# Two attention-and-routing stages on one core: the bank sum before the pair's last sum, the copy before a relu, and another order in the first item

## The chip, the cores and the metric

One core of a Trainium2 chip runs the whole program in one launch. The time is the device time of one execution in microseconds (us). The times shown are the median of several executions on the chip, and one further execution was recorded with its profile.

## The reference, cut to what matters

```python
x = attention(q, k, v, S1, S2)                  # (4352, 128): polynomial-sketch attention
P = exp(x @ w_gate - max)                       # 4352 x 8 gates
for _ in range(8):                              # Sinkhorn: rows, then columns
    P /= P.sum(1, keepdims=True) + 1e-09
    P /= P.sum(0, keepdims=True) + 1e-09
    P *= N / E
for e in range(8):                              # every token through every expert
    h = np.maximum(x @ w1[e], 0.0)              # 128 -> 1024
    out += P[:, e:e + 1] * (h @ w2[e])          # 1024 -> 128
```

Everything is fp32. All eight experts see all 4352 tokens, so the expert part is two dense products per token and expert.

## The kernel before, in words

**Two phases.** Up to about 194 us of the profile the kernel does the attention, the gates and some expert work (`steps`, lines 779 to 824). From then on `weighted` (lines 953 to 1262) does the rest: 60 *items*, each a group of tokens with one expert. The gate is multiplied into x ahead of the first layer, which a relu lets through because gates are positive.

**Groups, items and halves.** `wgroups` (line 592) has ten groups of tokens. Groups 0 to 4 have two blocks of 256 tokens and seven experts, groups 5 to 7 two blocks of 224 and six, group 8 five and group 9, `LAST`, two. An item is run in two *halves* (s = 0 and 1: which half of the hidden columns). `todo` (line 960) lists the halves as t = 0, 1, 2 and so on, so item 0 is t = 0 and 1, and item 1 is t = 2 and 3.

**Two layers, interleaved.** The loop at line 1240 runs `firsts(t)`, the first layer of half t, against `seconds(t - 1)`, the second layer of the half before, one `yield` of each in turn. A *slot* below is one such turn on TensorE: eight matmul records of the profile, either of line 986 (first layer) or of line 1124 (second layer). Seven first-layer slots and seven second-layer slots make a half.

**Fewer products by sums (groups 1 to 8 in both layers, items 1 and up in the first).** The first layer of a half has two token blocks and two column blocks, which need eight block products. `firsts` does seven, of sums of weights (`w1x`, eight forms; `sum_first` makes four of them on GpSimd once per expert) and of sums of tokens (`xf`, eight forms; `sum_x` makes four of them per item, in three parts). The seven go by turns into two PSUM tiles, `pairs[0]` and `pairs[1]`, called `pa` and `pc` in a half. ScalarE copies three partial results out (`p1`, `p5`, `u2`; lines 1061, 1067, 1070), and VectorE adds them back (`add`, line 990): h0 after the fourth product, h2 after the fifth, **h3, the pair's last sum, after the sixth**. ScalarE does the relu (line 993) of h0, of h2 and, after the seventh, of h1. VectorE then makes four sums for the second layer from h1 and h3 (lines 1086, 1095, 1096, 1097). Since `pa` and `pc` swap with t, the first product of half t + 1 goes into the tile that h3's add of half t reads.

**Item 0 is direct.** Its sums of weights aren't made yet, so it does eight plain products (lines 1047 to 1059): four results of two products each, with a relu on ScalarE after each second one. In item 0 the tiles alternate within a half and swap between halves as everywhere, so the last result of t = 0 and the first of t = 1 share a tile, and so do the last of t = 1 and the first product of t = 2.

**The end of a group.** The second layer adds up in four PSUM banks, `acc[g][rho][q]`. The next group uses the same four banks, so its first second-layer slot waits until they are read. For groups 1 to 8, while `seconds` runs the group's last half in slots 0 to 6, `firsts` of the next group's first half runs beside it. After second-layer slot 3 `ended(g, 0)` copies bank (0, 0) to the tile `z` on ScalarE (line 1170), and `ending` holds g. At first-layer slot 5 `add_half(g, 0)` adds bank (1, 0) to it on VectorE (line 1175): this is **the bank sum**. The other two banks follow at the end (`ended(g, 1)`, `add_half(g, 1)`). Group 0, whose second layer is direct, does all of this in its last slot. `z` has one buffer. `finish_seven` puts nine adds that read z and a swapped copy of it on a list, `leisure`, and later halves do them one at a time, on VectorE in `spare` and on GpSimd in `aside`.

**Queues.** Each engine runs its instructions in the order in which `weighted` writes them, SyncE its DMAs too. SyncE's queue around item 0 is: the swapped copy of item 2's x (`weigh`, line 904), the store of expert 1's weight sums (`store_form`, line 887, two parts), the load of w2 for item 1 (`prepare(1, True)`, line 860), the store of item 1's first sums (line 887), and the load of w1 for item 2 (line 856, four DMAs). Each store waits for GpSimd's sums; each DMA behind it in the queue waits with it. The ACT copies of line 1003 are one column wide and only hold GpSimd's work back until a point of the half (`gate`).

Of the kernel before, what the change touches and what calls it, by code (L numbers as in the profile page):

```python
# [50 lines left out]
def kernel(  # L51
# [825 lines left out]
    def sum_second(i):  # L877
        _, w2, ws = forms[i]
        g = nc.gpsimd
        four = [ws[:, n].rearrange("p (r s) d -> p r s d", r=2) for n in range(4)]  # L880
        g.tensor_tensor(four[0], block_of(w2, 1, 0), block_of(w2, 1, 1), op=Alu.add)
        g.tensor_tensor(four[1], four[0], block_of(w2, 0, 0), op=Alu.subtract)
        g.tensor_tensor(four[2], block_of(w2, 1, 0), block_of(w2, 0, 0), op=Alu.subtract)
        g.tensor_tensor(four[3], block_of(w2, 0, 1), four[1], op=Alu.subtract)

    def store_form(i, which):
        nc.sync.dma_start(out=form_stores[witems[i][1]][which], in_=forms[i][2 * which])
# [65 lines left out]
    def weighted():  # L953
# [16 lines left out]
        def firsts(t):  # L970
# [1 line left out]
            i, s = todo[t]  # L972
            g, e = witems[i]
            n = wgroups[g][1]
            a, c = pairs[t % 2], pairs[1 - t % 2]
            w1, xf = forms[i][0], sources[i]
            h, ts = rooms(t)
            pa, pc = a[:, :, 0:n], c[:, :, 0:n]
# [10 lines left out]
            def add(out, x, y):  # L989
                nc.vector.tensor_tensor(flat(out, n), x, flat(y, n), op=Alu.add)  # L990

            def relu(x, y):
                nc.scalar.activation(out=x, in_=y, func=Act.Relu)  # L993
# [11 lines left out]
            def aside(y):  # L1005


                if s == 0 and i + 2 < len(witems):
                    weigh(i + 2, lambda x: gate(x, y))
                if s == 1 and i + 1 < len(witems) and g:  # L1010
                    gate(sources[i + 1][:, 4, 0:1], y)
                    sum_x(i + 1, 0)
                if g == 0:
                    nexts = i + 1 < len(wgroups[0][2])
                    if s == 0:
                        if nexts:
                            gate(forms[i + 1][0][:, 4, 0:1], y)
                            sum_first(i + 1)
                        if i == 0:
                            sum_first(0)  # L1020
                            sum_second(0)
                            store_form(0, 0)
                        store_form(i, 1)
                    elif nexts:
                        gate(forms[i + 1][2][:, 0, 0, 0:1], y)
                        sum_second(i + 1)
                        store_form(i + 1, 0)
                elif chores and (s or not leisure):
                    chores.pop(0)[1]()
                else:  # L1030
                    leave(nc.gpsimd)
# [15 lines left out]
            if i == 0:  # L1047
                for out, (fi, ti), b in ((pa, (0, 1), 0), (pc, (1, 0), 1), (pa, (1, 1), 2), (pc, (0, 0), 3)):
                    for k in range(2):
                        product(out, 2 * k + fi, 2 * k + ti, k == 0, True)  # L1050
                        if k:
                            relu(flat(h[:, b], n), out)
                        if b == 0 and k:
                            aside(h[:, b, 0:1])
                        if b == 3 and k:
                            for part_ in ((1, 2) if s else (0,)):
                                sum_x(1, part_)
                        yield
                return
# [12 lines left out]
            yield  # L1072
            product(pc, 7, 3, False, True)
            add(h[:, 0], pc, u2)
            relu(h[:, 0], h[:, 0])
            yield
            product(pa, 6, 5, False, True)
            add(h[:, 2], pa, p5)
            relu(h[:, 2], h[:, 2])
            yield  # L1080
            product(pc, 2, 2, True, True)
            add(h[:, 3], pc, p1)
            if g in whole:
                relu(h[:, 3], h[:, 3])
            else:
                nc.vector.scalar_tensor_tensor(ts[:, 0], h[:, 3], 0.0, h[:, 0], op0=Alu.max, op1=Alu.subtract)  # L1086
            if ending:
                add_half(ending[0], 0)
            else:
                spare(0)  # L1090
            yield
            product(pa, 3, 7, False, True)
# [147 lines left out]
        for t in range(len(todo) + 1):  # L1240
            if t < len(todo):
                i, s = todo[t]
                g0 = witems[i][0]
                if s == 0:
                    prepare(i + 1, False)
                    if i + 3 < len(witems):
                        load_weights(i + 3)
                    if i == 0:
                        chores += chores_of(0) + chores_of(1)
                    if i and witems[i - 1][0] < g0 and g0 + 1 < LAST:  # L1250
                        chores += chores_of(g0 + 1)
                else:
                    prepare(i + 1, True)
            f = firsts(t) if t < len(todo) else iter(())
            s = seconds(t - 1) if t else iter(())
            nothing_, open_ = object(), 2
            while open_:
                open_ = sum(next(x, nothing_) is not nothing_ for x in (f, s))
# [108 lines left out]
```

## Time and profile before

| | |
|---|---|
| median of 3 executions | 911.18 us (910.59 to 912.69) |
| the profiled execution's own time | 910.05 us |
| its span, first to last instruction | 908.3 us |
| TensorE granted clock | 1.00 of full speed |
| VectorE, ScalarE, GpSimd busy | 721.9, 548.9, 245.2 us |
| TensorE weight loads busy | 703.5 us |
| HBM read and written | 137.24 and 19.57 MB |

In the timeline a row is: start, duration, engine, line, operation, output and inputs, shape, and in brackets the idle time of the engine just before and what ended it. Neighbouring instructions of one kind are merged (x8 is eight of them). The waits view has: engine and line, what it waited for, total us, times, longest. TensorE's matmuls overlap one another, so the idle time that a row shows is less than the time lost; the distance between equal instructions of two halves gives the loss. The copy of u2 (line 1070) comes once in each half, a fixed distance behind the third first-layer slot, and serves as such a beat.

### The profile page before, as it was taken

How to read it: one execution, taken by the hardware profiler on the slowest of the kernel's cores; microseconds unless marked ns; L12 is line 12 of the kernel's file. 1: busy time of each engine (PE TensorE's matmuls, PEld its weight loads, DVE VectorE, ACT ScalarE, POOL GpSimd, SP SyncE). 2: the span in 40 equal slices, each digit the busy share in tenths (PEclk: the TensorE clock that was granted, in tenths of full speed). 3: DMA queues.
4: the chain of work that ended last, by engine and by line, in shares of the span. 5: the costliest groups of instructions: out<-in, count | busy, mean ns of one | idle time of the engine just before them, and what ended most of it. 6: DMA issues, size and time to landing. Idle time of an engine off the chain costs nothing.

```text
span 908.3 us, 35879 instructions
## 1 busy us (share of the span) xinstructions
PE 895.1 (99%) x15484; PEld 703.5 (77%) x15484; DVE 721.9 (79%) x1268; ACT 548.9 (60%) x1092; POOL 245.2 (27%) x297
## 2 busy tenths in 40 slices
PE   9999999999999999999999999999999999999997
PEld 5777644557887766788877777888999978999996
DVE  7578789874445888888888888888898888888885
ACT  2446465646665666666666666666666666666664
POOL 3121100045652322233223222222233222233220
PEclk9999999999999999999999999999999999999999
DMA  8996200148885676485757667755884974875863
GB/s 240 291 277 201 54 1 1 49 110 290 265 239 194 219 240 198 128 268 189 223 183 236 182 205 208 240 190 152 257 258 129 291 257 117 275 242 165 281 202 90
DMA packets 124782, 177.98 MB, mean 196 GB/s; under 512 B 28976, under 2 KB 94720, under 8 KB 117584
## 3 DMA queue, kind: packets, MB, share of 16 engines
q1 hardware_dynamic: 121920, 170.18, 60.4%
q0 software_dynamic: 1600, 5.36, 2.1%
q8 instruction: 122, 2.00, 0.9%
q10 hardware_dynamic: 1104, 0.15, 0.1%
q14 instruction: 36, 0.29, 0.1%
HBM read 137.24 MB, written 19.57 MB: 173 GB/s over the span
## 4 chain that ended last, share of the span: by engine, by line
PE 84%; issue 10%; DVE 2%; POOL 1%; DMA 1%; ACT 1%; SPq 0%; POOLq 0%; DVEq 0%; ACTq 0%
PE s L1124 37%; PE pair L986 36%; PE a L711 4%; PE s L772 3%; PE a L305 1%; PE a L118 1%; PE a L420 1%; DMA w<-in_moe_w_dram 1%; DVE hb L990 1%; DVE hb L1086 1%; DVE z L1175 0%; PE a L272 0%; DMA pb<-pT 0%; PE s L334 0%; POOL xf L901 0%
## 5 line engine op out<-in xcount | busy, mean ns | idle before, releaser
L986 PE MATMUL pair<-xf,w1x 64*64 64x256 f32 (+1 forms) x6736 | 603.4, 366 | 2.0 <-ACT xf L1003 1.0
L986 PEld LDWEIGHTS pair<-xf,w1x 64*64 64x64 f32 x6736 | 337.8, 133 | 55.7 <-ACT hb L993 1.9
L990 DVE TENSOR_TENSOR hb<-pair,copies 128x512 f32<-128x512 f32 (+1 forms) x354 | 234.7, 663 | 127.7 <-PE pair L986 53.4
L1124 PE MATMUL s<-hb,w 64*64 64x256 f32 (+1 forms) x3600 | 312.4, 366 | 3.4 <-DVE z L1175 2.8
L1124 PE MATMUL s<-hb,ws 64*64 64x256 f32 (+1 forms) x3264 | 300.6, 364 | 0.0
L993 ACT ACTIVATE hb<-hb 128x512 f32<-128x512 f32 (+1 forms) x252 | 153.3, 609 | 112.2 <-DVE hb L990 107.6
L1124 PEld LDWEIGHTS s<-hb,w 64*64 64x64 f32 x3600 | 185.0, 133 | 38.7 <-PE pair L986 4.0
L1124 PEld LDWEIGHTS s<-hb,ws 64*64 64x64 f32 x3264 | 180.7, 133 | 27.7
L901 POOL TENSOR_TENSOR xf<-xT,pb 128x512 f32<-128x512 f32 (+1 forms) x60 | 75.2, 1254 | 302.1 <-ACT xf L1003 213.3
L910 POOL TENSOR_TENSOR xf<-xf 128x512 f32<-128x512 f32 (+1 forms) x52 | 63.1, 1213 | 229.7 <-ACT xf L1003 169.6
L711 PE MATMUL a<-xT,w 128*64 128x416 f32 (+3 forms) x512 | 121.2, 466 | 0.0
L713 ACT ACTIVATE hb<-a 128x416 f32<-128x416 f32 (+3 forms) x128 | 59.7, 468 | 68.7 <-PE a L711 56.7
L993 ACT ACTIVATE hb<-pair 128x512 f32<-128x512 f32 (+1 forms) x126 | 72.3, 573 | 38.0 <-PE pair L986 37.9
L1067 ACT COPY copies<-pair 128x512 f32<-128x512 f32 (+1 forms) x118 | 66.5, 563 | 36.6 <-PE pair L986 36.6
L1070 ACT COPY copies<-pair 128x512 f32<-128x512 f32 (+1 forms) x118 | 66.4, 563 | 30.7 <-PE pair L986 30.7
L1061 ACT COPY copies<-pair 128x512 f32<-128x512 f32 (+1 forms) x118 | 66.6, 565 | 27.8 <-PE pair L986 27.8
L726 DVE TENSOR_TENSOR hb<-hb 128x416 f32<-128x416 f32 (+7 forms) x84 | 59.5, 709 | 21.1 <-ACT hb L713 15.2
L1086 DVE SCALAR_TENSOR_TENSOR hb<-hb 128x512 f32<-128x512 f32 (+1 forms) x102 | 67.8, 665 | 10.6
L772 PE MATMUL s<-hb,ws 128*64 128x416 f32 (+3 forms) x224 | 70.9, 475 | 0.3
L711 PEld LDWEIGHTS a<-xT,w 128*64 128x64 f32 x512 | 49.9, 137 | 24.8 <-issue 15.9
L1095 DVE TENSOR_TENSOR hb<-hb 128x512 f32<-128x512 f32 (+1 forms) x102 | 66.5, 652 | 1.7
L1097 DVE TENSOR_TENSOR hb<-hb 128x512 f32<-128x512 f32 (+1 forms) x102 | 66.8, 655 | 0.0
(180 smaller groups left out, 669.4 us busy)
## 6 DMA issues: line engine op xcount, KB each, us to landing
w1x<-w1x SPq DMA_DIRECT2D x52, 1024.0 KB, 6.5
w<-in_moe_w_dram SPq DMA_DIRECT2D x56, 512.0 KB, 4.6
ws<-ws SPq DMA_DIRECT2D x52, 512.0 KB, 5.2
pb<-pT SPq DMA_DIRECT2D x35, 256.0 KB, 5.3
xf<-xf SPq DMA_DIRECT2D x70, 128.0 KB, 2.8
pb<-pT SPq DMA_DIRECT2D x25, 224.0 KB, 6.8
xf<-xf SPq DMA_DIRECT2D x50, 112.0 KB, 2.8
w1x<-in_moe_w_dram SPq DMA_DIRECT2D x28, 128.0 KB, 5.6
```

The lines of the kernel that those rows point to most:

```text
L711: nc.tensor.matmul(ph[sl], loaded_w[j][0][:, P * f + H2 * s:P * f + H2 * (s + 1)], xT[:, at + lo:at + hi], start=True, stop=True, tile_pos ...
L772: nc.tensor.matmul(sums[g][i][H2 * s:H2 * (s + 1)], w, x, start=c == 1, stop=c == per, tile_position=(0, H2 * s))
L901: nc.gpsimd.tensor_tensor(xf[:, 0:2].rearrange("p b n -> p (b n)"), xT[:, lo:lo + 2 * n], weights.pop(i), op=Alu.mult)
L986: nc.tensor.matmul(out[H2 * col:H2 * (col + 1), r], w1[rows, form, o:o + H2], xf[rows, x], start=start, stop=stop, tile_position=(H2 * r, ...
L990: nc.vector.tensor_tensor(flat(out, n), x, flat(y, n), op=Alu.add)
L993: nc.scalar.activation(out=x, in_=y, func=Act.Relu)
L1061: nc.scalar.copy(flat(p1, n), pa)
L1067: nc.scalar.copy(flat(p5, n), pc)
L1086: nc.vector.scalar_tensor_tensor(ts[:, 0], h[:, 3], 0.0, h[:, 0], op0=Alu.max, op1=Alu.subtract)
L1095: nc.vector.tensor_tensor(ts[:, 2], h[:, 1], ts[:, 0], op=Alu.subtract)
L1097: nc.vector.tensor_tensor(ts[:, 3], h[:, 2], ts[:, 2], op=Alu.subtract)
L1124: yield lambda rho=rho, rows=rows, c=c: nc.tensor.matmul(acc[g][rho][q][H2 * half:H2 * (half + 1), n * place:n * (place + 1)], w[rows], fl ...
```

## The change

Five edits, four of them in item 0 or at a group's end:

- **The order of the pairs (line 975).** For item 0 the tiles no longer swap between halves: both halves use `pairs[0]` first. Item 1 on alternates as before.
- **w2 of item 1 (lines 1019 and 1253).** `prepare(1, True)` is called inside `aside` of t = 0, ahead of `store_form(0, 0)`, instead of at the start of t = 1.
- **Sums of x for item 1 (line 1056).** All three parts are written at the end of t = 0, instead of one at t = 0 and two at t = 1. They are VectorE's first three instructions of `weighted` either way.
- **The relu of h0 (line 1075).** It is written behind the `yield`, so behind the second-layer slot 3 of the same turn. Where that slot ends a group's first two banks, `ended(g, 0)` comes ahead of the relu in ScalarE's order. Elsewhere ScalarE's order stays.
- **The bank sum (line 1087).** `add_half` comes ahead of h3's add in VectorE's order instead of behind h3's add and line 1086.

```diff
-            a, c = pairs[t % 2], pairs[1 - t % 2]
+            a, c = pairs[::-1] if t % 2 and i else pairs
...
                             sum_second(0)
+                            prepare(1, True)
                             store_form(0, 0)
...
-                            for part_ in ((1, 2) if s else (0,)):
+                            for part_ in range(0 if s else 3):
...
             add(h[:, 0], pc, u2)
+            yield
             relu(h[:, 0], h[:, 0])
-            yield
...
             product(pc, 2, 2, True, True)
+            if ending:
+                add_half(ending[0], 0)
             add(h[:, 3], pc, p1)
...
-            if ending:
-                add_half(ending[0], 0)
-            else:
+            if not ending:
                 spare(0)
...
-                else:
+                elif i:
                     prepare(i + 1, True)
```

## The prediction, on record before the result

> **What bounds the kernel now.** First the head of the page, then who waits for whom on TensorE.
>
> ```profile
> span 908.3 us, 35879 instructions
> PE 895.1 (99%) x15484; PEld 703.5 (77%) x15484; DVE 721.9 (79%) x1268; ACT 548.9 (60%) x1092; POOL 245.2 (27%) x297
> ...
> PE s L1124 <- DVE z L1175: 2.8, 7, 1.2
> PE pair L986 <- ACT hb L993: 0.7, 1, 0.7
> ```
>
> TensorE is the bound in every stage, so the change is worth what it takes from TensorE's stalls, and little else. The stalls it aims at are there: seven waits for the bank sum (L1175, one of them the 1.2 us of group 0, whose bank sum is not moved) and one for a relu. Their sums understate the loss, since matmuls overlap. The beat of L1070, one per half, gives the loss.
>
> ```profile
> 374.25 0.58 ACT L1070 COPY copies<-pair 128x512 f32<-128x512 f32 x1 [0.28 <-PE pair L986]
> 381.06 0.59 ACT L1070 COPY copies<-pair 128x512 f32<-128x512 f32 x1 [0.28 <-PE pair L986]
> 387.11 0.59 ACT L1070 COPY copies<-pair 128x512 f32<-128x512 f32 x1 [0.28 <-PE pair L986]
> ...
> 695.11 0.53 ACT L1070 COPY copies<-pair 128x448 f32<-128x448 f32 x1 [0.22 <-PE pair L986]
> 701.18 0.53 ACT L1070 COPY copies<-pair 128x448 f32<-128x448 f32 x1 [0.22 <-PE pair L986]
> ...
> 825.68 0.53 ACT L1070 COPY copies<-pair 128x448 f32<-128x448 f32 x1 [0.23 <-PE pair L986]
> 831.75 0.53 ACT L1070 COPY copies<-pair 128x448 f32<-128x448 f32 x1 [0.23 <-PE pair L986]
> ```
>
> An undisturbed half of 256-token blocks takes 387.11 - 381.06 = 6.05 us, so a slot (14 to the half) takes 0.432 us. The half with group 1's end takes 6.81: 0.76 lost. With 224-token blocks a slot takes 0.378 (the matmul rows of group 5 below: 0.37 and 0.38 per slot), a half 5.29, and the halves with the ends of groups 5 and 7 take 6.07 each: 0.78 lost. Group ends thus cost 0.76 to 0.78 us each. That is the stock from which the second part of the change can draw; the first draws from the start of this phase.
>
> **Part 1, item 0.** The rows are TensorE's, ScalarE's, SyncE's and GpSimd's around t = 0 to 4.
>
> ```profile
> 194.21 3.83 PE L986 MATMUL pair<-xf,w1x 64*64 64x256 f32 x64
> 198.75 0.66 PE L986 MATMUL pair<-xf,w1x 64*64 64x256 f32 x8 [0.72 <-ACT hb L993]
> 206.22 0.66 PE L986 MATMUL pair<-xf,w1x 64*64 64x256 f32 x8 [0.33 <-POOL ws L882]
> 212.72 0.64 PE L986 MATMUL pair<-xf,w1x 64*64 64x256 f32 x8
> 213.72 0.66 PE L1124 MATMUL s<-hb,w 64*64 64x256 f32 x8 [0.37 <-DMA w<-in_moe_w_dram]
> ...
> 197.24 0.60 ACT L993 ACTIVATE hb<-pair 128x512 f32<-128x512 f32 x1 [0.40 <-PE pair L986]
> 198.10 0.60 ACT L993 ACTIVATE hb<-pair 128x512 f32<-128x512 f32 x1 [0.27 <-PE pair L986]
> ...
> 197.63 1.12 SPq L904 DMA_DIRECT2D xf<-xf  x2
> 207.92 0.39 SPq L860 DMA_DIRECT2D w<-in_moe_w_dram  x1
> ...
> 218.62 0.73 POOL L870 TENSOR_TENSOR w1x<-w1x 128x256 f32<-128x256 f32 x1 [0.73 <-DMA pb<-pT]
> 221.05 0.73 POOL L873 TENSOR_TENSOR w1x<-w1x 128x256 f32<-128x256 f32 x1
> ```
>
> *Order of the pairs.* t = 0's eight products end at 198.04, and t = 1's first starts at 198.75: it shares its tile with t = 0's last result, whose relu ends at 198.10 + 0.60 = 198.70, 0.05 before. With one order it takes the tile of the result before, whose relu ends at 197.24 + 0.60 = 197.84, so it starts at 197.89: 0.86 us gained. t = 1 is 16 slots of 0.432, 6.91 us, so t = 2 can start at 197.89 + 6.91 = 204.80 instead of 206.22. Its tile was read two slots of products earlier, so no wait takes the place. (The row names GpSimd's ws as releaser; the code has no such dependence for this product. The relu of the shared tile is the one that fits.) Both boundaries together: **1.42 us**. What is late next is t = 2's second product, which needs the relu of t = 1's last result. That comes some 0.9 us after the last product and the second product three slots (1.3 us) after it: no wait.
>
> *w2 of item 1.* The second-layer slot at 213.72 was due one slot after 212.72, at 213.15: **0.57 us** lost to w2, whose load SyncE issued at 207.92, behind two stores. In its new place it goes out behind the x copies, at 197.63 + 1.12 = 198.75, and needs the same 5.8 us or less: landed by 204.6, eight us ahead of use. The stores come 0.4 us later in the queue at most, and nothing but later loads waits for them. GpSimd's next sums (L881), which had waited for the same load, can move up with it.
>
> *Sums of x.* They are VectorE's first three instructions before and after: 0.
>
> *What could take it back.* TensorE reaches t = 4 two us earlier, and its fourth product there needs the weight sums of item 2 that end at 221.05 + 0.73 = 221.78. Now t = 4's fourth product is due at about 222.4 (t = 2's first plus two halves of 6.48, its 15 slots, plus three turns of 0.86, from 206.22 with the 0.57: 222.3), so there are 0.6 us to spare against 2.0 gained. These sums wait for the load of item 2's w1 (the bracket of 218.62 names another DMA of that queue; the code waits for w1). That load went out right behind w2's 512 KB, which itself stood behind two stores of 1.5 MB and took 5.8 us; with a quarter of these 2 MB gone from ahead of it, it should come some 1.5 us sooner (an estimate), and GpSimd is free earlier. So from 0 to 1.4 us could be lost; I take 0, since the load moves up by about what is needed. Part 1: 1.42 + 0.57 = **2.0 us** (0.6 to 2.0).
>
> The Trainium skill's page "DMA: Bandwidth & Descriptors", section "Queues, rings and completion order", says that each DMA engine consumes a queue's descriptors in ring order. By that rule the w1 load of item 2 must come sooner once w2 isn't ahead of it, and the lost 1.4 us can't be; the 5.8 us of w2 behind the stores agrees.
>
> **Part 2, the group's end.** First group 1.
>
> ```profile
> 375.91 0.63 ACT L993 ACTIVATE hb<-hb 128x512 f32<-128x512 f32 x1 [0.81 <-DVE hb L990]
> 376.45 0.57 ACT L1170 COPY z<-s 128x512 f32<-128x512 f32 x1
> ...
> 375.98 0.69 DVE L990 TENSOR_TENSOR hb<-pair,copies 128x512 f32<-128x512 f32 x1
> 376.85 0.69 DVE L990 TENSOR_TENSOR hb<-pair,copies 128x512 f32<-128x512 f32 x1 [0.17 <-PE pair L986]
> 378.25 0.68 DVE L1175 TENSOR_TENSOR z<-s,z 128x512 f32<-128x512 f32 x1
> 378.85 0.68 DVE L1095 TENSOR_TENSOR hb<-hb 128x512 f32<-128x512 f32 x1
> ...
> 379.08 0.43 PE L1124 MATMUL s<-hb,w 64*64 64x256 f32 x2 [0.34 <-DVE z L1175]
> ```
>
> h3's add (376.85) follows its product's end (376.80) at once. Second-layer slot 3 ended three slots before, at 375.50. ScalarE then sat idle until 375.91 for h0. **The copy** can start at 375.55 and end at 376.12, and h0's relu follows 0.3 us later than now, which no one needs before the next half. **The bank sum** follows h2's add (375.98; VectorE starts independent sums 0.60 apart, 378.25 to 378.85): 376.58 instead of 378.25. The wait at 379.08 is gone.
>
> What is late next is **h3**: behind the bank sum it starts at 377.18, 0.33 later, and ends at 377.87. The next half's first product goes into the tile that h3 reads. It is due four slots after the start of h3's product (376.80 - 0.64 + 1.73 = 377.89), and VectorE's end reaches TensorE 0.15 later (378.25 + 0.68 to 379.08), at 378.02: a new stall of 0.13, with 0.1 for the restart say 0.2. So 0.76 becomes 0.2: 0.55 gained. Groups 1 to 4: 4 x 0.55 = **2.2 us**. The new wait is nowhere in the trace of before; its bounds are 0 (h3 in time) and the 1.7 of group 7 below.
>
> Groups 5 and 6 have shorter slots, and so less room:
>
> ```profile
> 698.18 0.66 PE L986 MATMUL pair<-xf,w1x 64*64 64x224 f32 x8
> 698.55 0.64 PE L1124 MATMUL s<-hb,w 64*64 64x224 f32 x4
> 699.41 0.41 PE L1124 MATMUL s<-hb,w 64*64 64x224 f32 x2 [0.21 <-DVE z L1175]
> ...
> 695.93 2.07 DVE L990 TENSOR_TENSOR hb<-pair,copies 128x448 f32<-128x448 f32 x3 [0.29 <-ACT xf L1003]
> ```
>
> The three adds end at 698.00; h2's begins at 696.62 (a turn of 0.76 before h3's). With 0.54 between sums (0.60 scaled by 0.62/0.69) the bank sum starts at 697.16, h3 at 697.70 and ends at 698.32; TensorE sees it at 698.47, while the product was due at 698.18: 0.29, with the restart 0.4 instead of 0.78. Gain 2 x 0.38 = **0.76 us**.
>
> **Group 7 goes the other way.**
>
> ```profile
> 827.78 0.66 POOL L1183 TENSOR_TENSOR y<-t,z 64x224 f32<-64x224 f32 x1
> ...
> 828.47 0.53 ACT L1170 COPY z<-s 128x448 f32<-128x448 f32 x1 [0.73 <-POOL y L1183]
> ...
> 828.75 0.67 PE L986 MATMUL pair<-xf,w1x 64*64 64x224 f32 x8
> ```
>
> The copy writes z, and GpSimd still reads group 6's z until 828.44; the change doesn't move that. The bank sum, now ahead of h3, holds VectorE until the copy's end at 829.00: bank sum 829.04, h3 829.58 to 830.20, TensorE at 830.35. The product that ran at 828.75 then stalls 1.6 us, 1.7 with the restart, instead of the 0.78 lost there now: **-0.9 us**.
>
> At the end of group 8 h3 has a relu of its own:
>
> ```profile
> 882.83 0.53 ACT L993 ACTIVATE hb<-pair 128x448 f32<-128x448 f32 x1
> ...
> 882.49 0.67 PE L986 MATMUL pair<-xf,w1x 64*64 64x224 f32 x8
> 884.27 0.61 PE L986 MATMUL pair<-xf,w1x 64*64 64x224 f32 x8
> ...
> 880.25 2.07 DVE L990 TENSOR_TENSOR hb<-pair,copies 128x448 f32<-128x448 f32 x3
> ```
>
> Now the two turns from 882.49 take 1.78 against 1.51: 0.27 lost. With h3 0.33 later (882.02 to 882.65) the product of 882.49 waits until 882.8, h1's relu (882.83) moves to 883.2 and the product behind it waits again until 883.8, and so does the copy after: some 0.7 in all, **-0.45 us**.
>
> Part 2: 2.2 + 0.76 - 0.9 - 0.45 = **1.6 us**. Bounds: if the tile is always free in time, 4 x 0.76 + 2 x 0.78 - 1.35 = 3.2; if h3's lateness costs what the bank wait cost, -1.35.
>
> A rule of the Trainium skill speaks against this part: "VectorE: DVE Perf Modes", section "The DRAIN you can't avoid", has the next VectorE instruction start only when the one before has left the pipe (and excepts ones that aren't held). By it sums would start 0.69 (0.62) apart, h3 would come up to 0.18 later at each of these ends, and part 2 would be about 0.4. The trace differs: 0.60 apart with 0.68 each.
>
> **Sum.** 2.0 + 1.6 = 3.6 us off the profiled execution's 910.05 us (span 908.3 and 1.75 around it): 906.5. The median of the runs is 1.13 above that execution, so on the median's scale 911.18 - 3.6 = **907.6**.
>
> **Rivals.**
> *A, the copy doesn't get ahead* (the change doesn't do what it says): if ScalarE's copy stays at 376.45 to 377.02, the bank sum starts at 377.06, h3 ends at 378.35 and the tile's stall, 0.6 with restart 0.7, replaces the bank's 0.76. Against it: ScalarE's idle 0.81 ahead of 375.91, long after the banks' last matmul. Groups 1 to 6 give nothing, 7 and 8 cost 1.35: 911.18 - 2.0 + 1.35 = 910.5.
> *B, weight sums of item 2 hold t = 4*: part 1 gives 0.6 only, part 2 its 1.6: 909.0. For it: 0.6 us of slack now. Against: that load has less ahead of it.
> *C, slower: VectorE held by the bank sum at every end*, as in group 7, the copy waiting for readers of z. Each of seven ends would cost 0.9 more than now, group 8 0.45 more: 911.18 - 2.0 + 6.8 = 916.0. It decides from the point where the copy ends after about 377.1 in group 1's terms (h3 then 0.6 late, all the bank's wait given back). Against it: at group 1 the copy followed the relu with no idle time; only group 7's row names a reader of z.
>
> **Chances.** Forecast 0.60; A 0.14; B 0.10; C 0.08; another stall moved by the earlier schedule, either sign, 0.08. Range: from 911.18 - 2.0 - 3.2 and 0.9 more should group 7 cost nothing, 905.1, up to A with the spread of single runs, 911.0. About 0.2% (1.8 us) is what a measurement here can tell from no change. Faster by more (below 909.4): forecast, B and part of the rest, 0.74. Within: A and some rest, 0.16. Slower: C and a little, 0.10.
>
> **What would show it.** Right: the first product of t = 1 near 197.9 and that of t = 2 near 204.8; no DMA wait at 213; the halves with the ends of groups 1 to 6 lose 0.2 to 0.4, with waits of L986 for DVE hb L990 in place of L1124 for DVE z L1175; group 7's half loses about 1.7. Wrong: a wait for weight sums at t = 4 (B), a relu ahead of the copy at 376 (A), waits of DVE for ACT z L1170 at many ends (C). The 1.2 us wait at group 0's end stays in every case.

## The result, and the profile after

The changed kernel takes **907.13 us** (median, 907.09 to 908.63); the kernel before, beside it, 911.31 (910.59 to 915.66). The ratio is 0.9949, with a 95% interval of 0.9925 to 0.9974, so 2.4 to 6.8 us less. The prediction was 907.6 (905.0 to 911.0). A second set of the same two kernels gave 907.06 against 910.80, ratio 0.9958 (0.9943 to 0.9972). The profiled execution after took 907.09 us, 2.96 less than the one before.

The head of the page after, whose line numbers from 1022 on are one higher (from the bank sum's new place to its old one, three):

```profile
span 905.3 us, 35878 instructions
...
PE 892.8 (99%) x15484; PEld 651.1 (72%) x15484; DVE 722.8 (80%) x1268; ACT 550.0 (61%) x1092; POOL 243.5 (27%) x297
```

And TensorE's waits after (engine and line, what it waited for, total us, times, longest):

```profile
PE s L1125 <- issue: 1.2, 1, 1.2
PE pair L986 <- DVE hb L990: 1.2, 1, 1.2
PE s L1125 <- DVE z L1176: 1.2, 1, 1.2
...
PE pair L986 <- issue: 0.6, 1, 0.6
PE pair L986 <- DVE hb L1089: 0.3, 1, 0.3
PE s L1125 <- ACT z L1171: 0.2, 1, 0.2
PE pair L986 <- POOL w1x L873: 0.2, 1, 0.2
```

The seven waits for the bank sum are down to one, group 0's 1.2 us. The waits for w2 and for the shared tile's relu are gone. New are one 1.2 us wait for h3's add (group 7), a 0.2 us wait for the weight sums of item 2, 0.3 us at t = 40 that the view puts down to line 1089 (see "No loads of weights after group 4"), and two lines that end in "issue": TensorE waited for nothing that the profile shows. Such a stall isn't new in itself. The kernel before has one of 1.0 us at t = 89, which its waits view puts down to ScalarE's copy of line 1003, though that copy ended 0.48 us before TensorE went on.

The beat of the u2 copy (line 1071 now) says what each part was worth. A half is named by the beat that ends it: t = 3 is the stretch from the beat of t = 2 to that of t = 3. Differences are taken before rounding and can lie 0.01 from those of the rows. The rows of the start, in the timeline after:

```profile
194.06 4.34 PE L986 MATMUL pair<-xf,w1x 64*64 64x256 f32 x72
...
204.69 0.61 PE L986 MATMUL pair<-xf,w1x 64*64 64x256 f32 x8
...
207.10 0.59 ACT L1071 COPY copies<-pair 128x512 f32<-128x512 f32 x1 [0.28 <-PE pair L986]
213.57 0.59 ACT L1071 COPY copies<-pair 128x512 f32<-128x512 f32 x1 [0.28 <-PE pair L986]
220.25 0.58 ACT L1071 COPY copies<-pair 128x512 f32<-128x512 f32 x1 [0.28 <-PE pair L986]
227.17 0.58 ACT L1071 COPY copies<-pair 128x512 f32<-128x512 f32 x1 [0.28 <-PE pair L986]
```

t = 0 runs into t = 1 without a gap (72 matmuls in one row). From the phase's first product, 0.15 earlier than before, to the first beat it is 13.04 us; before it was 14.46: 1.41 won. The next half, t = 3, takes 6.48 (before 7.07): 0.60 won. Then the two halves t = 4 and 5 take 6.67 and 6.93 instead of 6.48 each: 0.65 lost.

The rows of the ends of groups 1, 5 and 7:

```profile
372.74 0.58 ACT L1071 COPY copies<-pair 128x512 f32<-128x512 f32 x1 [0.28 <-PE pair L986]
373.82 0.59 ACT L1171 COPY z<-s 128x512 f32<-128x512 f32 x1 [0.23 <-PE s L1125]
375.07 0.68 DVE L1176 TENSOR_TENSOR z<-s,z 128x512 f32<-128x512 f32 x1
375.67 0.68 DVE L990 TENSOR_TENSOR hb<-pair,copies 128x512 f32<-128x512 f32 x1
376.41 0.66 PE L986 MATMUL pair<-xf,w1x 64*64 64x256 f32 x8
378.86 0.59 ACT L1071 COPY copies<-pair 128x512 f32<-128x512 f32 x1 [0.28 <-PE pair L986]
...
691.37 0.53 ACT L1071 COPY copies<-pair 128x448 f32<-128x448 f32 x1 [0.22 <-PE pair L986]
693.96 0.62 DVE L990 TENSOR_TENSOR hb<-pair,copies 128x448 f32<-128x448 f32 x1
694.63 0.61 PE L986 MATMUL pair<-xf,w1x 64*64 64x224 f32 x8
696.82 0.53 ACT L1071 COPY copies<-pair 128x448 f32<-128x448 f32 x1 [0.22 <-PE pair L986]
...
821.73 0.53 ACT L1071 COPY copies<-pair 128x448 f32<-128x448 f32 x1 [0.22 <-PE pair L986]
824.52 0.53 ACT L1171 COPY z<-s 128x448 f32<-128x448 f32 x1 [1.99 <-POOL y L1184]
825.08 0.62 DVE L1176 TENSOR_TENSOR z<-s,z 128x448 f32<-128x448 f32 x1 [1.22 <-ACT z L1171]
825.62 0.61 DVE L990 TENSOR_TENSOR hb<-pair,copies 128x448 f32<-128x448 f32 x1
826.29 0.61 PE L986 MATMUL pair<-xf,w1x 64*64 64x224 f32 x8 [1.23 <-DVE hb L990]
828.48 0.53 ACT L1071 COPY copies<-pair 128x448 f32<-128x448 f32 x1 [0.23 <-PE pair L986]
```

Group 1's half falls from 6.81 to 6.13 us (groups 2 to 4 by the same 0.68), group 5's from 6.07 to 5.45 (group 6 too, 0.63), and group 7's rises from 6.07 to 6.76. Group 8's, not shown, rises from 5.58 to 5.88.

The account of the two profiled executions: start -0.15, item 0 -1.41 and -0.60, t = 4 and 5 +0.65, ends 4 x -0.68 - 2 x 0.63 + 0.68 + 0.31 = -2.99; that makes -4.5. The last beat comes 2.91 earlier. The missing 1.6 is, on balance, in the halves t = 39 and 40 (0.58 longer than before) and 86, 87 and 89 (1.46 longer). In the last two TensorE stood still on "issue". Where that comes from is the subject of the last experiments.

### The profile page after: what moved, and what is told of

The parts are those of the page before. It is cut to its first block, busy times and chain, and to the rows that moved or that the text cites. A ratio compares the mean times of both kernels' runs of the same rounds, so it can differ in the third digit from the quotient of the medians.

```text
span 905.3 us, 35878 instructions
## 1 busy us (share of the span) xinstructions
PE 892.8 (99%) x15484; PEld 651.1 (72%) x15484; DVE 722.8 (80%) x1268; ACT 550.0 (61%) x1092; POOL 243.5 (27%) x297
## 4 chain that ended last, share of the span: by engine, by line
PE 92%; DVE 3%; DMA 2%; SPq 1%; issue 1%; ACT 0%; POOL 0%; DVEq 0%; ACTq 0%; POOLq 0%
PE s L1125 38%; PE pair L986 37%; PE a L711 7%; PE s L772 6%; PE a L305 1%; PE a L118 1%; PE a L420 1%; DVE hb L726 1%; DMA pb<-pT 1%; DMA w<-in_moe_w_dram 0%; PE a L272 0%; DVE hb L990 0%; DMA xf<-xf 0%; PE s L334 0%; SPq L856 0%
## 5 line engine op out<-in xcount | busy, mean ns | idle before, releaser
L986 PE MATMUL pair<-xf,w1x 64*64 64x256 f32 (+1 forms) x6736 | 527.7, 365 | 2.3 <-DVE hb L990 1.2
L986 PEld LDWEIGHTS pair<-xf,w1x 64*64 64x64 f32 x6736 | 277.5, 133 | 87.5 <-DVE hb L990 4.5
L1125 PE MATMUL s<-hb,w 64*64 64x256 f32 (+1 forms) x3600 | 275.6, 366 | 1.4 <-DVE z L1176 1.2
L1125 PE MATMUL s<-hb,ws 64*64 64x256 f32 (+1 forms) x3264 | 258.4, 364 | 1.2 <-issue 1.2
L1125 PEld LDWEIGHTS s<-hb,w 64*64 64x64 f32 x3600 | 149.2, 133 | 46.4 <-DVE z L1176 1.6
L1125 PEld LDWEIGHTS s<-hb,ws 64*64 64x64 f32 x3264 | 141.2, 133 | 36.6
```

The costliest lines, as they stand in the source:

```text
L986: nc.tensor.matmul(out[H2 * col:H2 * (col + 1), r], w1[rows, form, o:o + H2], xf[rows, x], start=start, stop=stop, tile_position=(H2 * r, ...
L1125: yield lambda rho=rho, rows=rows, c=c: nc.tensor.matmul(acc[g][rho][q][H2 * half:H2 * (half + 1), n * place:n * (place + 1)], w[rows], fl ...
```

## Experiments

Times are compared with the kernel before, run beside each set (medians 910.68, 910.34, 910.80 and 910.66; single executions 907.66 to 915.12). The halves are far steadier than the times, so both are given. Halves with a group's end, in us, from the beats of each trace:

| kernel | groups 1 to 3 | 5 and 6 | 7 | 8 |
|---|---|---|---|---|
| before, twice; item 0 alone; before without loads | 6.81 | 6.07 | 6.07 | 5.58 |
| after, twice; ends alone; other bank; load ahead; after without loads | 6.13 | 5.45 | 6.76 (ends alone and other bank 6.77) | 5.88 |
| bank sum alone | 6.60 | 5.92 | 6.76 | 6.35 |
| copy alone | 6.81 | 6.07 | 6.91 | 5.58 |
| two z | 6.13 | 5.45 | 5.45 | 5.88 |
| together | 6.13 | 5.45 | 5.45 | 5.58 |

**Theory**: the gain is the sum of the two parts, each where the prediction put it; TensorE's loss at an end is how late h3's add comes to the next half's first product. **Rivals**: the gain sits in one part alone; one of the two engines' orders does it alone; and the stalls named "issue" are part of the change's effect.

### Item 0 alone

```diff
-            a, c = pairs[t % 2], pairs[1 - t % 2]
+            a, c = pairs[::-1] if t % 2 and i else pairs
...
+                            prepare(1, True)
...
-                            for part_ in ((1, 2) if s else (0,)):
+                            for part_ in range(0 if s else 3):
...
-                else:
+                elif i:
```

> The kernel before with the three edits of the first item alone; the groups' ends as before. Theory: the first part gives 1.42 us at t = 0 and 1, and 0.57 at t = 2, as predicted, but the weight sums of item 2 give 0.65 back at t = 4 and 5 (by the trace of after): 1.35 us less than before, so about 909.9 on a median of 911.2; the first product of t = 2 near 204.8, the halves t = 4 and 5 together 13.6 instead of 12.95, the halves with group ends 6.81 (groups 1 to 4) and 6.07 (5 to 7) as before. Rival 1, the prediction's own size, nothing given back: 2.0 less, 909.2. Rival 2, what is won in the first 30 us is lost again behind it (loads that come no sooner): 911.2.

909.63 us, ratio 0.9987 (0.9975 to 0.9998): 0.2 to 2.3 less. In its trace the 1.41 and the 0.60 are there again, to 0.01 us. But t = 4 and 5 take 6.48 each: nothing is given back here. So the prediction's 2.0 is what this part does at its best, and my revised 1.35 rested on a single trace. The time can't tell 1.35 from 2.0; the halves can.

### The groups' ends alone

```diff
             add(h[:, 0], pc, u2)
+            yield
             relu(h[:, 0], h[:, 0])
-            yield
...
+            if ending:
+                add_half(ending[0], 0)
             add(h[:, 3], pc, p1)
```

> The kernel before with the order at the groups' ends alone (bank sum ahead of h3's sum, copy ahead of h0's relu); the first item as before. Theory, with the sizes that the halves of after show: 4 x 0.68 + 2 x 0.63 - 0.68 - 0.31 = 3.0 us less, about 908.2. The prediction's own sizes: 1.6 less, 909.6. Rival: the gain of the two kernels sits in the first item and the ends only shift stalls from the bank to the pair's tile: 911.2, with group halves back at 6.8.

908.86 us, ratio 0.9974 (0.9962 to 0.9986): 1.3 to 3.5 less. The halves at the ends are those of the changed kernel to 0.01 us, so this part is worth 2.99 by itself, and the first rival falls. Its trace also has "issue" stalls of 1.96 us (t = 87), 1.15 (t = 112) and 0.56 (t = 115) more than before, and one of 0.82 less (t = 89).

One more thing showed by chance. The half with w2's wait, written as before here, takes 6.53, against 7.07 in the trace of before. Over the six traces with the old first item it loses 0.05, 0.18, 0.20, 0.32, 0.60 and 0.96. So the 0.57 was one draw of a load's landing.

### One engine's order alone

The bank sum ahead of h3 on VectorE, the copy still behind h0's relu on ScalarE:

```diff
+            if ending:
+                add_half(ending[0], 0)
             add(h[:, 3], pc, p1)
...
-            if ending:
-                add_half(ending[0], 0)
-            else:
+            if not ending:
                 spare(0)
```

> The kernel before with the bank sum ahead of h3's sum on VectorE, but the copy still behind h0's relu on ScalarE. Theory (both moves are needed): the copy ends at 377.02 in group 1's terms as before, the bank sum starts at 377.06 and h3 ends at 378.35, so a stall of 0.6 to 0.7 for the pair's tile takes the place of the bank's 0.76: group halves 6.7 to 6.8, nothing won at groups 1 to 6, 0.68 and 0.31 lost at 7 and 8; about 911.2 to 912.2. Rival 1, VectorE's order alone does it: 3.0 less, 908.2. Rival 2, the third case of the prediction (VectorE held at every end): up to 916.

911.07 us, ratio 1.0004 (0.9991 to 1.0017). Group 1 in its timeline:

```profile
378.00 0.57 ACT L1170 COPY z<-s 128x512 f32<-128x512 f32 x1
...
378.60 0.69 DVE L1175 TENSOR_TENSOR z<-s,z 128x512 f32<-128x512 f32 x1 [0.38 <-ACT z L1170]
379.21 0.68 DVE L990 TENSOR_TENSOR hb<-pair,copies 128x512 f32<-128x512 f32 x1
```

This execution runs 1.55 us behind the one before at that place. In its terms the bank sum starts at 377.05 and h3 ends at 378.34: the prediction's rival A, which gave 377.06 and 378.35. VectorE waits 0.38 for the copy, and the pair's tile takes over the bank's stall. The half loses 0.55 instead of 0.76, so the ends win 0.21 and 0.16 where I had expected nothing, and lose 0.69 and 0.77 at groups 7 and 8: in all the ends cost 0.3 us more than before.

The copy ahead of h0's relu, the bank sum where it was:

```diff
             add(h[:, 0], pc, u2)
+            yield
             relu(h[:, 0], h[:, 0])
-            yield
```

> The kernel before with the copy ahead of h0's relu on ScalarE, but the bank sum still behind h3's sums on VectorE. Theory: the bank sum cannot start before VectorE's sum ahead of it has, and it starts 0.60 behind that as before (378.25 in group 1's terms), so nothing is won: 911.2 within 0.3, group halves 6.81 and 6.07. Rival, ScalarE's order alone does it: 3.0 less, 908.2.

912.32 us, ratio 1.0021 (1.0011 to 1.0031): 1.0 to 2.8 more. Group 1:

```profile
374.22 0.58 ACT L1170 COPY z<-s 128x512 f32<-128x512 f32 x1 [0.23 <-PE s L1124]
...
375.72 0.69 DVE L990 TENSOR_TENSOR hb<-pair,copies 128x512 f32<-128x512 f32 x1 [0.17 <-PE pair L986]
376.52 0.69 DVE L1086 SCALAR_TENSOR_TENSOR hb<-hb 128x512 f32<-128x512 f32 x1
377.13 0.68 DVE L1175 TENSOR_TENSOR z<-s,z 128x512 f32<-128x512 f32 x1
```

The copy is done at 374.80, and the bank sum still comes at 377.13, behind h3's add and line 1086: nothing won at any end. At group 7 it loses 0.84: the copy waits there for GpSimd's reading of z, and h0's relu now waits behind the copy. That I had not expected, and it is about half of what the time shows. Its trace also has "issue" stalls (1.84 us more at t = 87, 0.89 less at t = 89) and 0.86 more at t = 40, but one trace can't show that these make up the rest of the medians' difference. So neither order gains anything by itself over all the ends: the copy must be early **and** the bank sum ahead.

### Two buffers for z

From here on each kernel is the changed one with one edit.

```diff
-                ends[g] = late[0].tile([P, 2, 2 * NW], F32, tag="z", name="z", bufs=1)
+                ends[g] = late[0].tile([P, 2, 2 * NW], F32, tag="z", name="z", bufs=2)
```

> The changed kernel with two buffers for z in place of one. Theory: at group 7 the copy waits for GpSimd's last reading of group 6's z (the copy began at 828.47 in before, behind that sum), and the bank sum, now ahead of h3, holds VectorE until then; with a buffer of its own the copy starts right after the bank's last matmul, and group 7's half falls from 6.755 to 5.45 as in groups 5 and 6, 1.3 us less than the changed kernel; the 1.2 us wait of L986 for DVE hb L990 goes. Rival: the copy is held by something else (ScalarE's order, the bank), and the half stays at 6.75. Stalls without a shown cause may lie elsewhere than in the changed kernel's trace.

905.80 us, ratio 0.9943 (0.9925 to 0.9961). Group 7's beats in its timeline:

```profile
820.68 0.53 ACT L1071 COPY copies<-pair 128x448 f32<-128x448 f32 x1 [0.22 <-PE pair L986]
...
826.13 0.53 ACT L1071 COPY copies<-pair 128x448 f32<-128x448 f32 x1 [0.22 <-PE pair L986]
```

5.45 us instead of 6.76, 1.31 less, to the hundredth what groups 5 and 6 take. Group 7's loss is the copy's wait for the reader of z, and nothing else. In this trace, too, t = 4 and 5 take 6.48 each.

### Group 0's sums in other banks

```diff
-                acc[g] = [[mps.tile([P, 512], F32, tag=f"s{2 * rho + q}", name="s") for q in range(2)]
+                acc[g] = [[mps.tile([P, 512], F32, tag=f"s{2 * rho + (q ^ (g == 0))}", name="s") for q in range(2)]
```

> The changed kernel with group 0's sums in the other two of the four banks, so that group 1's first products find free banks. Theory: at group 0's end TensorE waits for the copy and the bank sum of the only pair of banks in use (gaps of 0.62 and 1.54 us at 289.75 and 290.64); with the other banks both go, about 1.9 us less than the changed kernel (905.2 against 907.1). Rival: the instruction packet that arrives 2.55 us before the longer stall ends causes it, and then it stays.

904.66 us, ratio 0.9933 (0.9914 to 0.9951). The half at group 0's end:

```profile
285.36 0.59 ACT L1071 COPY copies<-pair 128x512 f32<-128x512 f32 x1 [0.33 <-PE pair L986]
...
291.78 0.59 ACT L1071 COPY copies<-pair 128x512 f32<-128x512 f32 x1 [0.28 <-PE pair L986]
```

6.42 us instead of 8.67: 2.25 won, more than the two gaps that I had added up (1.9). The one bank-sum wait that the change left was the largest of them all.

### Item 2's load ahead of the store

```diff
+                        if i == 1:
+                            store_form(1, 0)
                         store_form(i, 1)
...
-                        store_form(i + 1, 0)
+                        if i:
+                            store_form(i + 1, 0)
```

> The changed kernel with the store of item 1's w1 sums (1 MB) behind the load of item 2's w1 in SyncE's queue instead of ahead of it. Theory: the load, which waits for 1 MB of store ahead of it, comes 1 to 2.5 us sooner, GpSimd's sums of item 2 with it, and the halves t = 4 and 5 return from 6.67 and 6.93 to 6.48 each: 0.65 us less than the changed kernel. Rival 1: the load is held by its buffer (it cannot start before 209.7 whatever is ahead of it) and nothing changes. Rival 2: the store, moved back, delays the loads of w2 or of item 3, and the loss appears two halves later.

906.63 us, ratio 0.9962 (0.9944 to 0.9980): by the times not to be told from the changed kernel. Halves t = 4 and 5: 6.48 each, as expected. But so they are in two kernels without this edit, so the half alone proves nothing; the queue does. First the changed kernel, the 1 MB store, the load and the first of GpSimd's sums on it:

```profile
207.80 1.81 SPq L887 DMA_DIRECT2D w1x<-w1x  x1
209.70 3.22 SPq L856 DMA_DIRECT2D w1x<-in_moe_w_dram  x4
...
217.87 0.73 POOL L870 TENSOR_TENSOR w1x<-w1x 128x256 f32<-128x256 f32 x1 [6.40 <-DMA xf<-xf]
```

Then the kernel with two z, whose program is the same here:

```profile
207.69 0.37 SPq L887 DMA_DIRECT2D w1x<-w1x  x1
208.36 3.83 SPq L856 DMA_DIRECT2D w1x<-in_moe_w_dram  x4
...
215.82 0.73 POOL L870 TENSOR_TENSOR w1x<-w1x 128x256 f32<-128x256 f32 x1 [4.46 <-ACT hb L993]
```

And the kernel with the load ahead:

```profile
208.78 2.95 SPq L856 DMA_DIRECT2D w1x<-in_moe_w_dram  x4
...
214.29 0.73 POOL L870 TENSOR_TENSOR w1x<-w1x 128x256 f32<-128x256 f32 x1 [2.50 <-DMA w1x<-in_moe_w_dram]
```

From the load's issue to the sums it is 8.2 us behind the store, 7.5 behind a store that was issued quickly, and 5.5 without one ahead. SyncE needs 0.37 us or 1.8 us for the same store's issue, and the loss goes with it: in three traces of the new first item the store took 1.81 to 2.03 and 0.65 to 0.72 was lost (the changed kernel, other bank, no loads); in three it took 0.37 and nothing was lost (item 0 alone, two z, the repetition below). It isn't the store alone: in the repetition the first load behind it took 2.02 to issue, and the sums came 10.0 us after the beat of t = 2, against 10.8 in the changed kernel and 8.8 with two z. Why an issue takes the one or the other stays open. With the old first item t = 4 and 5 lose 0 to 0.39 in six traces, so not all of the 0.65 is the change's.

### No loads of weights after group 4

```diff
-        return 0 < i < len(witems) and witems[i - 1][1] == witems[i][1]
+        return 0 < i < len(witems) and (witems[i - 1][1] == witems[i][1] or witems[i][0] > 4)
```

> The changed kernel with no loads of weights from group 5 on: every item there uses the weights that are in place, so its result leaves out the experts' own weights, and TensorE's instructions are the same. Theory: TensorE's stalls that no releaser explains (0.92 us at 717.80, 1.59 at 724.64 in the changed kernel; up to 2.29 in the parts) end 2.3 to 2.9 us after a 16 KB packet of the instruction queue that came 7 us or more behind the one before it: its instructions arrive late while the weights' loads fill the DMA engines. Without the loads no such stall is left after 690 us, all halves there without a group's end take 5.30, and the time is 1.5 to 2 us less, with less spread. Rival: these stalls come from TensorE or its clock, and stay.

902.87 us (902.65 to 903.56), ratio 0.9919 (0.9901 to 0.9938). One of the stalls, in the changed kernel's timeline:

```profile
726.23 0.35 PE L1125 MATMUL s<-hb,ws 64*64 64x224 f32 x1 [1.25 <-issue]
```

The DMA view of the changed kernel has no packet of queue q8 (instructions, 16 KB each) from 717.2 to 723.6 us, and one in the 2.6 us before this stall's end; queue, kind, packets, MB, share of the engines:

```profile
q1 hardware_dynamic: 150, 0.91, 92.1%
q8 instruction: 1, 0.02, 2.9%
```

By the trace that packet starts at 723.64, 2.59 us ahead of the restart. It is the rule: in the fourteen traces (both kernels, every experiment) 27 stalls of this phase are named "issue" and have matmul starts over 0.6 us apart, and all 27 end 2.26 to 2.66 us after the start of such a packet. Three more, which the profile puts down to a ScalarE copy (t = 89 of the kernel before, t = 115 in two traces), end 2.42 to 2.86 after one. These packets come about every 6.6 us, so chance would put some 3 of the 30 there. The same half without the loads:

```profile
722.50 0.53 ACT L1071 COPY copies<-pair 128x448 f32<-128x448 f32 x1 [0.22 <-PE pair L986]
727.79 0.53 ACT L1071 COPY copies<-pair 128x448 f32<-128x448 f32 x1 [0.22 <-PE pair L986]
```

5.30 us. From t = 75 to 115 every half without a group's end takes that, but for t = 80 (5.38 in every trace), where the changed kernel has 5.80, 6.16 and 6.86: 3.0 us less over those halves. So the loads make these stalls; the rival (TensorE or its clock) falls. That it is TensorE's instructions that come late behind them is inferred from the packets' times: no view shows which instructions a packet holds, or when it was asked for.

The loss at t = 40 is of another kind. There, where weights are still loaded, it stays (6.42 for 6.04). In three traces (item 0 alone, copy alone, the repetition) the profile names the load of ws, the second layer's weight sums, and TensorE goes on 0.04 us after its last semaphore update. The row of copy alone:

```profile
441.00 0.66 PE L1124 MATMUL s<-hb,ws 64*64 64x256 f32 x8 [0.62 <-DMA ws<-ws]
```

In four others (the changed kernel, ends alone, load ahead, no loads) it is the first product of t = 40 that comes late, 0.13 to 0.14 us after the last update by the load of its w1. So at t = 40 TensorE waits for the weights themselves, and no instruction packet is needed to explain it. In the changed kernel that product starts at 443.48; the view puts its wait down to line 1089.

### All of it, and the repetition

The changed kernel with two z, other banks and the load ahead, and group 8's bank sum back behind h3:

```diff
-            if ending:
+            if ending and g < LAST:
                 add_half(ending[0], 0)
...
+            if ending and g == LAST:
+                add_half(ending[0], 0)
```

> The changed kernel with two buffers for z, group 0's sums in the other banks, the 1 MB store behind the load of item 2's w1, and the bank sum of group 8 (where h3 has a relu of its own) back behind h3. Theory: 1.31 (group 7's half) + 2.25 (group 0's end) + 0.65 (t = 4 and 5) + 0.31 (group 8's half back to 5.58) = 4.5 us less than the changed kernel where that loses at t = 4 and 5, 3.9 where it doesn't: 902.6 to 903.3 against its 907.1. Halves with ends: 6.13, 5.45 and, at group 8, 5.58. Rival: what is won ahead makes the late instruction packets after 700 us cost more (up to 1 us each by the runs so far), and the total is 1 to 2 us less good.

**902.63 us**, ratio 0.9917 (0.9892 to 0.9942), 4.4 less than the changed kernel beside it. Every half came as expected: 6.42 at group 0's end, 6.48 at t = 4 and 5, 6.13, 5.45 (group 7 too), 5.58 at group 8's. The last beat comes 4.56 earlier than in the changed kernel's trace. Its waits of this phase are all "issue":

```profile
PE pair L986 <- issue: 1.1, 2, 0.7
...
PE s L1130 <- issue: 1.0, 1, 1.0
```

The changed kernel once more:

> The changed kernel once more, unchanged, for what a repetition differs by. Theory: halves with the groups' ends come out the same within 0.01 us (6.13, 5.45, 6.76, 5.88); the halves t = 4 and 5 lose 0.65 only if SyncE's issue of the 1 MB store ahead of item 2's load takes 1.8 us or more instead of 0.4; the stalls after 7 us between instruction packets come in the same halves (t = 40, 86, 87, 89, 112 to 115) with other sizes. Rival: the stalls without a releaser have the same sizes as in the first trace, so they belong to the program and not to the moment.

907.06 us. The halves with ends are the same to 0.01 us. t = 4 and 5 take 6.48, with a store issued in 0.37. Of the "issue" stalls, those of t = 87 and 89 come again with the same size (6.16 and 6.86 us, also in the kernel with the load ahead), while t = 86, 112 and 113 differ (5.31, 5.82 and 6.99 against 5.80, 5.32 and 5.30), and so does the wait for weights at t = 40 (6.72 against 6.54). So theory and rival each hold in part: some are set by the program's timing, the rest by the moment.

### Do the late instructions take part of the gain?

That left a doubt. Added up over the halves without a group's end from t = 16 on, above the shortest that any trace shows for each half, the excess was 2.20 us in the trace of before and 3.80 in that of after, 5.64 in the repetition. (Of these 0, 0.58 and 0.78 lie at t = 39 and 40, where TensorE waits for weights.) The last two kernels are the one before without loads after group 4 (the same one-line edit as above) and the one before once more.

> The kernel before with no loads of weights from group 5 on, as was done with the changed kernel: every item there uses the weights in place, so its result leaves out the experts' own weights. It answers whether the late instructions are part of the change's effect. Seven traces with the copy and the bank sum moved lose 3.4 to 5.6 us (4.5 in the mean) in halves without a group's end from t = 16 on, the four others 2.2 to 3.8 (3.1). Theory now: with TensorE less held at the ends, the late instructions cost about 1.4 us more, so the change is worth more without the loads than with them: 4.3 to 5.0 us by the halves, that is 907.2 to 907.9 against the 902.87 of the changed kernel without loads, a difference above the 3.7 to 4.2 with them. Rival: the two sets of traces differ by chance; then the excess is the same for both and the difference of the two kernels without loads is the 3.7 to 4.2 seen with them: 906.6 to 907.1.

907.33 us (906.31 to 908.55), ratio 0.9962 (0.9948 to 0.9977). Between the two kernels without loads lie 4.5 us of their medians (in their traces, 3.65 to the last beat). But they ran in different sets, whose kernels before took 910.34 and 910.66; each against its own, the difference is 4.1. The two longest of TensorE's waits in this phase:

```profile
PE s L1124 <- DVE z L1175: 2.8, 7, 1.2
...
PE pair L986 <- ACT hb L993: 0.7, 1, 0.7
```

The waits for the bank sums and for the shared tile's relu are there, none is named "issue", and t = 87 and 89 take 5.30 each.

> The kernel before once more, for a second trace. Halves with ends as before (6.81, 6.07, 6.07, 5.58) within 0.01. Theory: its halves without a group's end from t = 16 on lose less than 3.8 us in all, as in the four traces with an unmoved copy or bank sum, and less than the 4.5 of the moved ones. Rival: it lies among the moved ones (3.4 to 5.6), so the excess is the moment's alone. The time of the half with w2's wait, t = 3, is another draw between 6.5 and 7.4.

911.37 us, ratio 1.0000 (0.9990 to 1.0010). Its excess is 4.47 us, not 2.20: the kernel before has as much of it in another execution, and the rival holds for this run. The 4.5 us without loads are in the range of the theory, but the 4.1 against the kernels beside them is what the rival expected, the 3.7 to 4.2 with loads. So the theory that the change makes the late instructions cost more isn't borne out, and most of the 1.6 us that the first pair of traces didn't account for was the draw of those two traces. Whether a few tenths of the gain are given back in late instructions at every execution stays open.

## Why the prediction came out right, step by step

- **What bounds the kernel**: held. TensorE's stalls carry all of it, and the beat measures them; every end repeats to 0.01 us.
- **Order of the pairs, 1.42**: measured 1.41, in every trace with the edit. The profile had named GpSimd's ws as releaser of t = 2's first product; the reading by the code (the shared tile's relu) was the right one: in the trace after, that sum (line 882) starts only at 205.24, behind the product at 204.69.
- **w2, 0.57**: measured 0.60, but its size is a draw between 0.05 and 0.96, 0.39 in the mean of six traces. With the new order it is 0 in every trace.
- **Sums of x, 0**: no trace shows a wait there.
- **What could take it back, taken as 0 of 0 to 1.4**: the term that failed, 0.65 in the trace of after; 0 in half of the traces with the new first item. The load did not move up by the 1.5 us that I estimated: SyncE issued it at 209.70 (209.47 before), and the sums began 0.75 earlier. The ring order in the Trainium skill's page "DMA: Bandwidth & Descriptors", section "Queues, rings and completion order", is not contradicted by this: with fewer bytes ahead the sums did begin sooner. But the issue itself came late, so the prediction's sentence that by this rule the loss can't be was too strong.
- **Group's end, the instants**: right. In the terms of before (1.51 us later there) the bank sum starts at 376.58 and h3 at 377.18, ending at 377.86; I had 376.58, 377.18 and 377.87.
- **Groups 1 to 4, 0.2 left of 0.76, and 5 and 6, 0.4 left of 0.78: mis-sized**, 0.08 and 0.15 are left. I took 0.15 from VectorE's end to TensorE, from a wait of the second layer, and 0.1 for a restart, for which I had no row. From h3's end to the waiting product it is 0.05 to 0.06 (376.35 to 376.41, 694.58 to 694.63, 826.23 to 826.29). The restart costs about 0.05: at group 7 the slot ahead of the product starts at 824.51, so with slots 0.38 apart the product was due at 824.89; it starts at 826.29, 1.40 late, the next slot follows at 826.72, 0.43 behind instead of 0.38, and the half loses 1.46. At group 5 the product is 0.11 late and the half loses 0.15. Lateness this short doesn't show in the waits view, so the waits for h3 that I had named as a sign at groups 1 to 6 aren't there. So 2.7 and 1.26 instead of 2.2 and 0.76.
- **Group 7, -0.9 and group 8, -0.45**: the right sign and cause, -0.68 and -0.31. The same two terms were too large. At group 8 the trace together, with the bank sum back behind h3 there, returns to 5.58, so that order is the cause.
- **Part 2, 1.6**: it is 2.99, near the upper bound of 3.2. With part 1's 2.0 the two parts make 5.0 where nothing is given back, not 3.6.
- **Why the time fits nonetheless**: the medians differ by 4.2 and, in the second set, 3.7; the profiled executions by 2.96. What the ends gave more was lost at t = 4 and 5, in a smaller w2 wait than that of the profiled execution, and, in the trace after, in the wait for weights at t = 40 and in "issue" stalls, two terms that the prediction didn't have. The time came within 0.5 us by two errors of opposite sign, not by exact terms.
- **The rules and rivals**: A (the copy does not get ahead) did not occur, and the bank sum alone showed what it would have been, a loss of 0.55 at group 1 where I had 0.7. B came true by half in some traces. C holds at group 7 alone. The Trainium skill's rule in "VectorE: DVE Perf Modes", section "The DRAIN you can't avoid", read without its exception for instructions that aren't held, has sums start a full duration apart and would have made part 2 0.4; the trace has the bank sum and h3 0.60 apart with 0.68 each (375.07 and 375.67).

## What to carry to other kernels

Where two engines in a row free a tile, look at the order on both: one order alone gave nothing here or a loss, both gave 3.0 us, and the new order must be asked which buffer the first engine waits for (here z, worth 1.3 us). Measure such a change by the distance of equal instructions between neighbouring stretches, which repeats to 0.01 us, while the time of one kernel scatters by several us. A stall that names no releaser, in stretches where loads fill the DMA engines, is worth comparing with the instruction packets and with the landing of the loads before it is put down to the change.

## What the runs showed of the hardware that I had not expected

- TensorE restarts 0.05 to 0.06 us after the VectorE add that it waits for, and the half loses only some 0.05 us beyond the lateness (1.40 late and 1.46 lost at group 7).
- TensorE stalls of up to 2.3 us (start to start) that no wait explains end 2.3 to 2.7 us after the start of a 16 KB packet of the instruction queue (27 of 27 named "issue"). There are 122 such packets, 2.00 MB in an execution, 0.9% of the DMA engines' time. Without the weights' loads after group 4 none is left there.
- SyncE's issue of the same 1 MB store took 0.37 us in some executions of the new order and 1.8 to 2.0 in others.
- Over the experiments, whole executions of the kernel before lay between 907.66 and 915.12 us, while the halves that no load or instruction packet disturbs agree to 0.01.
